# The loads of Q, K and V on ScalarE's queue in place of SyncE's

## The chip, the cores and the metric

The kernel runs on one core of a Trainium2 chip. The metric is the device time of one execution in microseconds (us). The engines are TensorE (PE; its weight loads are PEld), VectorE (DVE), ScalarE (ACT), GpSimd (POOL) and SyncE (SP), which computes nothing and issues DMAs.

## The reference

Attention with a delta rule over 768 tokens, for 4 batches of 8 heads of size 48, then a mixture of 8 experts with a capacity, then a gated two-layer network over all 3072 tokens:

```python
for t in range(S):
    kt, vt, bt = (k_n[:, :, t], v[:, :, t], beta[:, :, t, None])
    y[:, :, t] = np.einsum('bhd,bhde->bhe', q[:, :, t], state)
    v_old = np.einsum('bhde,bhd->bhe', state, kt)
    state = state + bt[:, :, :, None] * np.einsum('bhd,bhe->bhde', kt, vt - v_old)
...
logits = x @ w_gate          # each token to one expert, at most N // E tokens each
h = np.maximum(x[mask] @ w1[e], 0.0); out[mask] = h @ w2[e]
...
h = x @ w_in; g = h * (1.0 / (1.0 + np.exp(-h))); y = g @ w_out
```

`k_n` is K divided by its norm along the head.

## The kernel before

The tokens are cut into 24 chunks of 32, and the state is carried from chunk to chunk. Numbers are split into pairs of float16 (a high and a low part), so each product takes three matmuls.

`prep(c)` loads a chunk's Q and K, transposed, in two halves of 128 x 512 float32 (256 KB each) into one of three `raw` buffers (line 351; the first four chunks are loaded whole, line 344) and splits each half: ACT makes the high part (L353), DVE the low part (L354). For a pair of chunks four DMAs then copy K inside SBUF into `gsl` (L359). `gram(c)` multiplies K and Q with K (L376). `tgroup(g)`, once for four chunks, solves a triangular system on DVE and POOL (L443 and L446, with L429, L449 and L458 around them). `stage(c)` loads K and V once more, not transposed, in one DMA of 384 KB into one of two buffers `kr` (line 466), splits K (L469 on ACT, L470 on DVE), scales V (L473), and then copies all the matmul weights of the chunk with four DMAs of 256 KB inside SBUF into `rsl[x]`, of which there are two (L482). `step(c)` is the recurrence: V goes into PSUM (L505), the old state is multiplied in (L513, L523), the result is split on ACT and DVE (L487, L488), more matmuls follow (L534, L549, L560), some splits use ACT twice (L492, L495), and every second chunk leaves by four DMAs (L572). `gate(c)` makes the expert logits. The MoE begins after the last chunk; it is bound by the matmuls of L1124. The conversion of `win` (L787 loads it) is spread through the end of attention.

No engine's order is written by hand. Every operation is given to `Plan.op` with an engine, a cost, what it reads and writes and a priority. `Plan.order` simulates the engines and puts all operations in one list by their planned starts; the engines then run their parts of it strictly in order. A DMA whose engine is SP also needs one of eight lanes in this plan:

```python
if o[6] and e == "SP":
    s = max(s, lanes[0])
```

The DMAs of SP, in the order in which they are issued, tell of their landing through eight semaphores in turn (DMAHW0 to DMAHW7 in the lists of instructions below). A DMA that takes over a semaphore waits until the one that had it before has landed.

Of the kernel before, what the change touches and what calls it, by code (L numbers as in the profile page):

```python
# [237 lines left out]
def dve(n):  # L238
    return 0.15 + 0.00104 * n


def act(n, sb=True):
    return 0.165 + 0.00083 * n + (0.03 if sb else 0.0)


def pool(n):
    return 0.22 + 0.0018 * n
# [6 lines left out]
def attention(tc, P, ar, sh, kq, kv, bt, cst, idh, wg, xs):  # L254
    nc = tc.nc
# [24 lines left out]
    kr = [ar.new([("kr", i), ("kv", i, 0)], [16, D]) for i in two]  # L280
# [25 lines left out]
    def nat(x, a, t):  # L306
        return NAT[x] + 2 * a + t

    def blk(h):
        return slice(32 * h, 32 * h + 32)  # L310

    def dma(nbytes, fn, r, w, cost=0.63, slots=None, **k):
        P.op("SP", cost, fn, r=r, w=w, lat=0.9, xfer=slots or nbytes / 360e3, **k)

# [13 lines left out]
    late = [("cp", 0, x, k) for x in two for k in ("h1", "l1")]  # L328
# [6 lines left out]
    def grams(c):  # L335
        return (rsl[1][:, 0:8].rearrange("p (x c) g s n -> p x c g s n", x=2), ("rsl", 1)) if c in (2, 3) else (gsl, "gsl")

    def prep(c):
        m, x = c // 2, c % 2
        gs, gk = grams(c)  # L340
        cr = [cpt[m % NR][:, x, r[x]:r[x] + 4].rearrange("p (l t) n -> p l t n", l=2) for r in (QR, KR)]
        ck = lambda k: ("cp", m % NR, x, k)
        if c < 4:
            dma(5.25e5, lambda e: nc.sync.dma_start(first[c][0].rearrange("p k n -> p (k n)"), kq[c]), [], first[c][1])
        for k in (1, 0):
            if c < 4:
                rt, rk = first[c][0][:, k], first[c][1]
            else:
                i = (2 * c + 1 - k) % 3
                rt, rk = raw[:, i], [("raw", i)]  # L350
                dma(2.62e5, lambda e, rt=rt, k=k: nc.sync.dma_start(rt, kq[c, :, 512 * k:512 * k + 512]), late if c < 8 else [], rk)
            rt = rt.rearrange("p (t n) -> p t n", t=2)
            P.op("ACT", act(512), lambda e, k=k, rt=rt: A.activation(cr[k][:, 0], rt, AF.Copy, scale=2.0 ** 9), r=rk, w=[ck(f"h{k}")])  # L353
            P.op("DVE", dve(512), lambda e, k=k, rt=rt: V.scalar_tensor_tensor(cr[k][:, 1], rt, 2.0 ** 9, cr[k][:, 0], op0=OP.mult,  # L354
                                                                               op1=OP.subtract), r=rk + [ck(f"h{k}")], w=[ck(f"l{k}")])
        if x:
            def slots(e):
                for h in range(4):
                    nc.sync.dma_start(gs[blk(h)].rearrange("p x c g s n -> p (x c g) s n")[:, :, h],  # L359
                                      cpt[m % NR][blk(h)].rearrange("p x c (g n) -> p (x c g) n", g=2)[:, 2 * KR[0]:2 * KR[0] + 16])  # L360
            dma(5.25e5, slots, [("cp", m % NR, y, k) for y in range(2) for k in ("h1", "l1")], [gk], cost=2.6, pieces=4, slots=2.5)
# [99 lines left out]
    def stage(c):  # L461
        gi = next(g for g, cs in enumerate(GROUPS) if c in cs)
        m, x = c // 2, c % 2
        cr, k_ = cpt[m % NR][:, x], kr[x]
        ck = lambda k: ("cp", m % NR, x, k)
        dma(3.93e5, lambda e: nc.sync.dma_start(k_.rearrange("p a d -> p (a d)"), kv[c]), late if c < 2 else [], [("kr", x), ("kv", x, 0)])
        hi, lo = (cr[:, nat(x, a, 0):nat(x, a, 2)].rearrange("p t (g n) -> p (t g) n", g=2)[:, :, 0:2 * D] for a in two)
        src = k_[:, 0:8].rearrange("p (b a) d -> p b (a d)", b=4)
        P.op("ACT", act(384), lambda e: A.activation(hi, src, AF.Copy, scale=2.0 ** 9), r=[("kr", x)], w=[ck("nh")])  # L469
        P.op("DVE", dve(384), lambda e: V.scalar_tensor_tensor(lo, src, 2.0 ** 9, hi, op0=OP.mult, op1=OP.subtract),  # L470
             r=[("kr", x), ck("nh")], w=[ck("nl")])
        vs = k_[:, 8:16]
        P.op({"DVE": dve(384), "Pool": pool(384)}, 0, lambda e: E[e].tensor_tensor(  # L473
            vs, vs, nrt[:, gi, c % 4, :, None].to_broadcast([128, 8, D]), op=OP.mult), r=[("nrt", gi)], w=[("kv", x, 0)])
        v2 = vhl[x]
        P.op("ACT", act(384), lambda e: A.activation(v2[:, 0], vs, AF.Copy), r=[("kv", x, 0)], w=[("kr", x)])
        P.op({"DVE": dve(384), "Pool": pool(384)}, 0, lambda e: E[e].tensor_tensor(v2[:, 1], vs, v2[:, 0], op=OP.subtract),
             r=[("kv", x, 0)], w=[("kr", x)])

        def slots(e):  # L480
            for h in range(4):
                nc.sync.dma_start(rsl[x][blk(h)].rearrange("p a g s n -> p (a g) s n")[:, :, h], cr[blk(h)].rearrange("p a (g n) -> p (a g) n", g=2))  # L482
        dma(1.05e6, slots, [ck(k) for k in ("h0", "l0", "h1", "l1", "n", "nh", "nl", "ph", "pl", "th", "tl")],
            [("rsl", x)], cost=2.6, pieces=4, slots=5.1)
# [145 lines left out]
    for c in range(NCH):  # L630
        if c % 2 == 0 and c + 5 < NCH:
            pair(c + 4)
        if c % 4 == 2 and c + 2 < NCH:
            at(c + 2, "tgroup")
            tgroup(c // 4 + 1)
        at(c, "stage")
        stage(c)
        at(c, "step")
        step(c)
        at(c, "gate")  # L640
        gate(c)
# [563 lines left out]
def _program(ins):  # L1205
    import concourse.bacc as bacc

    nc = bacc.Bacc("TRN2", target_bir_lowering=False, num_devices=1)
    d = {k: nc.dram_tensor(f"in_{k}", a.shape, mybir.dt.from_np(a.dtype), kind="ExternalInput").ap()
         for k, a in ins.items()}  # L1210
    out = nc.dram_tensor("out_0", _OUT, F32, kind="ExternalOutput").ap()
    with tile.TileContext(nc) as tc, ExitStack() as ctx:
        dram = ctx.enter_context(tc.tile_pool(name="dram", bufs=1, space=DRAM))
        xs = dram.tile([NTOK, 2 * DM], F16, name="xs")
        plan = Plan()
        ar = Arena(ctx, tc, plan, 212832)
        ar.at(210852)
        sh = shared_tiles(ar)
        ar.at(0)
        plan.base, plan.look = 9.0 * HOT, LOOK  # L1220
        attention(tc, plan, ar, sh, d["kq"], d["kv"], d["bt"], d["cst"], d["idl"], d["wg"], xs)
        moe(tc, plan, ar, sh, xs, d["w1"], d["w2"], d["win"], d["wout"], d["mch"], out)
        with tc.manual_schedule():
            plan.emit()
    return nc
# [22 lines left out]
```

## Time and profile before

| | |
|---|---|
| median of 3 runs | 1058.98 us (1054.76 to 1065.01) |
| the profiled execution's own time | 1058.44 us |
| its span, first to last instruction | 1056.7 us |
| mean granted TensorE clock | 0.934 |

The profiled execution is 0.5 us from the median, and 1.7 us of it lie outside the span. Attention fills about the first 370 us of the span: the last chunk's output is issued at 371 us. Between 350 and 400 us the search for the first expert begins.

### The profile page before, as it was taken

What the parts mean: (1) busy time and instruction counts of PE and PEld (TensorE: products, weight loads), DVE (VectorE), ACT (ScalarE), POOL (GpSimd) and SP (SyncE); (2) the same over time, 40 slices, a digit from 0 to 9 for tenths busy, and PEclk for the clock granted to TensorE, in tenths of its full rate; (3) what the DMA queues carried; (4) which work ended last, traced back from release to release, by engine and by line L of the source; (5) the groups of instructions that cost most, each with busy time, mean ns of one, the idle gap of its engine ahead of it and who ended that gap; (6) DMA issues with size and microseconds to landing.
All of it is one profiled execution on the core that took longest, in us unless ns stands there. A gap on an engine that the chain in (4) does not pass through costs nothing.

```text
span 1056.7 us, 26434 instructions
## 1 busy us (share of the span) xinstructions
PE 921.0 (87%) x10753; PEld 662.3 (63%) x10753; DVE 728.5 (69%) x1831; ACT 493.2 (47%) x992; POOL 444.2 (42%) x567
## 2 busy tenths in 40 slices
PE   7878789898888725987989998997999999999997
PEld 7767779888877613543655654654665666566664
DVE  5999999999974798997477468359459457542250
ACT  4414546464646634555445255236236346741250
POOL 6768676867643241674135035017016113112021
PEclk9987889899988956997999999999999999999999
DMA  7339787888869726213131022004004104401000
GB/s 219 106 77 199 166 190 170 199 190 192 186 158 195 176 76 232 90 61 106 59 105 46 16 63 87 16 10 137 20 1 127 39 1 150 135 1 38 8 1 23
DMA packets 178792, 107.63 MB, mean 102 GB/s; under 512 B 141680, under 2 KB 162416, under 8 KB 178672
## 3 DMA queue, kind: packets, MB, share of 16 engines
q1 hardware_dynamic: 175600, 96.52, 36.0%
q0 software_dynamic: 3072, 9.44, 2.7%
q8 instruction: 84, 1.38, 0.5%
q14 instruction: 36, 0.29, 0.1%
HBM read 65.04 MB, written 9.44 MB: 70 GB/s over the span
## 4 chain that ended last, share of the span: by engine, by line
PE 49%; DVE 23%; DMA 11%; SPq 6%; issue 5%; POOL 4%; ACT 3%; POOLq 0%; DVEq 0%; ACTq 0%
PE bank L1124 41%; SPq L482 4%; DMA sb<-sb 3%; DMA sb<-in_kq 3%; DVE sb L903 3%; DMA sb<-in_kv 2%; DVE sb L443 2%; DVE sb L1164 1%; DMA sb<-xs,sb 1%; DVE sb L1161 1%; DVE sb L446 1%; DVE sb L354 1%; PE bank L192 1%; DVE sb L488 1%; PE bank L376 1%
## 5 line engine op out<-in xcount | busy, mean ns | idle before, releaser
L1124 PE MATMUL bank<-sb 128*128 128x384 f16 x3456 | 591.1, 329 | 6.3 <-DVE sb L1164 5.0
L1124 PEld LDWEIGHTS <-sb 128*128 128x128 f16 x3456 | 327.5, 98 | 220.4 <-issue 8.4
L1164 POOL TENSOR_TENSOR sb<-sb 128x384 f16<-128x384 f32 x71 | 70.4, 996 | 273.1 <-ACT sb L1163 206.3
L1163 ACT ACTIVATE sb<-sb 128x384 f16<-128x384 f32 x128 | 66.1, 520 | 41.7 <-DVE sb L1161 41.1
L1161 DVE SCALAR_TENSOR_TENSOR sb<-bank,sb 128x384 f32<-128x384 f32 x128 | 70.0, 551 | 22.6 <-ACT sb L1160 18.2
L376 PE MATMUL bank<-sb 128*128 128x64 f16 x1152 | 75.3, 242 | 10.5 <-DVE sb L385 5.1
L1160 ACT ACTIVATE sb<-bank 128x384 f32<-128x384 f32 x128 | 61.3, 481 | 47.4 <-PE bank L1124 45.6
L376 PEld LDWEIGHTS <-sb 128*128 128x128 f16 x1152 | 72.8, 120 | 12.2 <-issue 11.0
L1173 POOL DMA_INDIRECT out<-sb x24 | 23.8, 990 | 119.9 <-ACT sb L1171 107.0
L446 POOL TENSOR_TENSOR sb<-sb 128x126 f32<-128x126 f32 (+22 forms) x146 | 68.9, 472 | 10.4
L443 POOL TENSOR_TENSOR sb<-sb 128x126 f32<-128x126 f32 (+22 forms) x146 | 68.1, 466 | 10.4
L443 DVE TENSOR_TENSOR sb<-sb 128x30 f32<-128x30 f32 (+23 forms) x180 | 65.7, 365 | 3.3
L446 DVE TENSOR_TENSOR sb<-sb 128x30 f32<-128x30 f32 (+23 forms) x180 | 63.1, 351 | 3.3
L488 DVE SCALAR_TENSOR_TENSOR sb<-bank,sb 128x192 f16<-128x192 f32 (+1 forms) x118 | 49.7, 426 | 21.1 <-ACT sb L487 20.8
L513 PE MATMUL bank<-sb 128*128 128x48 f16 x1104 | 46.2, 195 | 19.8 <-DMA sb<-sb 12.6
L487 ACT ACTIVATE sb<-bank 128x192 f16<-128x192 f32 (+1 forms) x118 | 45.4, 388 | 37.6 <-PE bank L513 18.7
L513 PEld LDWEIGHTS <-sb 128*128 128x128 f16 x1104 | 43.6, 117 | 23.1 <-issue 21.8
L903 DVE TENSOR_TENSOR sb<-sb 128x192 f16<-128x192 f16 (+3 forms) x116 | 55.3, 512 | 1.0
L1052 POOL TENSOR_TENSOR sb<-sb 128x768 f16<-128x768 f32 x26 | 47.1, 1825 | 20.9 <-ACT sb L1051 20.0
L549 PE MATMUL bank<-sb 128*128 128x48 f16 x1104 | 49.9, 196 | 6.5 <-ACT sb L487 3.8
L1134 ACT ACTIVATE sb<-bank 128x384 f16<-128x384 f32 x64 | 31.3, 489 | 50.7 <-PE bank L1124 46.7
L1135 DVE SCALAR_TENSOR_TENSOR sb<-bank,sb 128x384 f16<-128x384 f32 x64 | 35.3, 554 | 28.0 <-ACT sb L1134 27.9
(159 smaller groups left out, 1494.1 us busy)
## 6 DMA issues: line engine op xcount, KB each, us to landing
sb<-sb SPq DMA_DIRECT2D x96, 256.0 KB, 5.5
sb<-in_w SPq DMA_DIRECT2D x64, 384.0 KB, 4.0
sb<-in_kq SPq DMA_DIRECT2D x40, 256.0 KB, 4.1
sb<-in_kv SPq DMA_DIRECT2D x24, 384.0 KB, 5.2
sb<-sb SPq DMA_DIRECT2D x48, 128.0 KB, 2.7
sb<-in_win SPq DMA_DIRECT2D x8, 768.0 KB, 4.7
sb<-in_wout SPq DMA_DIRECT2D x8, 768.0 KB, 6.5
xs<-sb SPq DMA_DIRECT2D x48, 96.0 KB, 3.9
```

What stands on the lines that cost most here:

```text
L376: T.matmul(gp_[:, Q], sta(gs[:, x], 2 * a + t, Q), cv[:, :, b, t, Q // 4, :, Q % 4], start=(n == 0), stop=(n == 5))
L443: P.op(en, cost[en](n * m), lambda e, x=x, t=t, j=j, n=n, m=m: E[e].tensor_tensor(t, L[:, j:j + 1, j + 1:].to_broadcast([128, n, m]), x[:, ...
L446: P.op(en, cost[en](n * m), lambda e, x=x, t=t, j=j: E[e].tensor_tensor(x[:, :, j + 1:], x[:, :, j + 1:], t, op=OP.add), r=[("tmp", en)], ...
L488: P.op("DVE", dve(n), lambda e: V.scalar_tensor_tensor(lo, src, s, hi, op0=OP.mult, op1=OP.subtract), r=[r, wh], w=[wl])
L513: T.matmul(wu_[:, 0, Q], sta(rs, KR[x] + 2 * a + t, 4 * g + Q), n_[:, b, t, Q, :], start=False, stop=(last and (a, b) == P3[-1] and Q == 3 ...
L549: T.matmul(st_[:, t, Q], sta(rs, nat(x, a, t), 4 * g + Q), u_[:, b, Q], start=(c == 0 and n == 0 and Q == 0 and t == 0), stop=False, skip_ ...
L903: V.tensor_tensor(mv, a, iota2[:, None, 0:J].to_broadcast([128, h, J, 2]), op=o)
L1124: T.matmul(bk[:, :N], lw(a), rw(b), start=(first and n == 0), stop=(last and n == 2))
L1160: op("ACT", act(N, False), lambda e, bk=bk, y=y: A.activation(sg[y], bk[:, :N], AF.Sigmoid, scale=s3), [kbk], [("sg", y)])
L1161: v(dve(N), lambda e, bk=bk, y=y: V.scalar_tensor_tensor(gf[y], bk[:, :N], s3 * 2.0 ** SG, sg[y], op0=OP.mult, op1=OP.mult), [kbk, ("sg", ...
L1163: op("ACT", act(N), lambda e, f=f, y=y: A.activation(gT[:, 0, f], gf[y], AF.Copy), [("gf", y)], [("gT", f, 0)])
L1164: op({"DVE": dve(N), "Pool": pool(N)}, 0, lambda e, f=f, y=y: EN[e].tensor_tensor(gT[:, 1, f], gf[y], gT[:, 0, f], op=OP.subtract), [("gf" ...
```

## The change

The 40 half loads of Q and K (all but those of the first four chunks) and the 24 loads of K and V are issued by ACT. A new helper gives them to the plan at a cost of 0.1 us, where SP's DMAs had 0.63 us, and without lanes. What they load, their buffers and what they wait for stay. SP keeps the copies inside SBUF, the outputs and all loads of the MoE.

```diff
+    def load(nbytes, fn, r, w):
+        P.op("ACT", 0.1, fn, r=r, w=w, lat=0.9, xfer=nbytes / 360e3)
+
     def dma(nbytes, fn, r, w, cost=0.63, slots=None, **k):
         P.op("SP", cost, fn, r=r, w=w, lat=0.9, xfer=slots or nbytes / 360e3, **k)
...
-                dma(2.62e5, lambda e, rt=rt, k=k: nc.sync.dma_start(rt, kq[c, :, 512 * k:512 * k + 512]), late if c < 8 else [], rk)
+                load(2.62e5, lambda e, rt=rt, k=k: nc.scalar.dma_start(rt, kq[c, :, 512 * k:512 * k + 512]), late if c < 8 else [], rk)
...
-        dma(3.93e5, lambda e: nc.sync.dma_start(k_.rearrange("p a d -> p (a d)"), kv[c]), late if c < 2 else [], [("kr", x), ("kv", x, 0)])
+        load(3.93e5, lambda e: nc.scalar.dma_start(k_.rearrange("p a d -> p (a d)"), kv[c]), late if c < 2 else [], [("kr", x), ("kv", x, 0)])
```

Three lines are added, so a line L351 of before is L354 of the changed kernel, L353 is L356, L466 is L469, L469 is L472, L482 is L485, L487 is L490, and so on. Since the plan is made anew, all engines' orders change in attention; after it, from the expert search on, the five orders are the same as before. The numbers of instructions stay, but for the 64 DMAs and four small operations that the plan gives to another of their permitted engines.

SP's queue of the kernel before, from the output of chunks 0 and 1 (L572) past that of chunks 2 and 3 (the next L572):

```order
L572 DMA xs<-sb 32x8x192 x4
L351 DMA sb<-in_kq 128x512 x2
L359 DMA sb<-sb 32x16x128 x4
L466 DMA sb<-in_kv 128x768
L482 DMA sb<-sb 32x32x128 x4
L351 DMA sb<-in_kq 128x512 x4
L482 DMA sb<-sb 32x32x128 x4
L466 DMA sb<-in_kv 128x768
L572 DMA xs<-sb 32x8x192 x4
L466 DMA sb<-in_kv 128x768
L359 DMA sb<-sb 32x16x128 x4
L482 DMA sb<-sb 32x32x128 x4
```

The same place in the changed kernel, where L575 is the output, L362 the copy for `gsl` and L485 the copy for `rsl`:

```order
L575 DMA xs<-sb 32x8x192 x4
L362 DMA sb<-sb 32x16x128 x4
L485 DMA sb<-sb 32x32x128 x8
L575 DMA xs<-sb 32x8x192 x4
L362 DMA sb<-sb 32x16x128 x4
L485 DMA sb<-sb 32x32x128 x8
```

The copies of one chunk now follow those of the chunk before with nothing between them; the nine loads that stood among them are gone from this queue.

ACT's order of the kernel before, between the splits of the outputs of chunk 1 (bank 70) and chunk 2 (bank 69), with what each instruction waits for in brackets (an engine's name is that engine's semaphore):

```order
L487 ACTIVATE sb<-bank_67 128x192 [waits DVE_49,PE_49]
L492 ACTIVATE sb<-bank_68 128x192 [waits DVE_49,PE_49]
L389 ACTIVATE sb<-sb 128x256 [waits DVE_49]
L353 ACTIVATE sb<-sb 128x512 [waits DMAHW5_49,DMAHW4_49,DMAHW6_49,DMAHW3_49,DMAHW1_49]
L469 ACTIVATE sb<-sb 128x4x96 [waits DMAHW7_49]
L383 ACTIVATE sb<-bank_71 128x8x32 [waits PE_49]
L495 ACTIVATE sb<-bank_68 128x192 [waits PE_49]
L487 ACTIVATE sb<-bank_65 128x384 [waits Activation_49]
```

The same place in the changed kernel:

```order
L490 ACTIVATE sb<-bank_67 128x192 [waits DVE_49,PE_49]
L386 ACTIVATE sb<-bank_71 128x8x32 [waits DVE_49]
L495 ACTIVATE sb<-bank_68 128x192 [waits PE_49,Activation_49]
L392 ACTIVATE sb<-sb 128x256
L354 DMA sb<-in_kq 128x512 [waits DVE_49,Activation_49]
L356 ACTIVATE sb<-sb 128x512 [waits DMAHW6_49,DMAHW4_49,DMAHW7_49,DMAHW2_49,DMAHW0_49]
L472 ACTIVATE sb<-sb 128x4x96 [waits DMAHW1_49]
L386 ACTIVATE sb<-bank_71 128x8x32 [waits PE_49]
L354 DMA sb<-in_kq 128x512 [waits DMAHW3_49,DVE_49]
L490 ACTIVATE sb<-bank_65 128x384 [waits PE_49]
```

The eight semaphores of the DMAs now go round over the DMAs of both queues. Two loads stand among ACT's own operations. Both wait for DVE, the second one also for the DMA that had DMAHW3 before it, which may be one of SP's; behind it stands the split of the state (L490 on bank 65), for which the next chunk's matmuls wait.

## Rows read from the trace of the kernel before

**Rows 1.** The page, parts 1 (busy time, share, instructions) and 4 (the chain).

```profile
PE 921.0 (87%) x10753; PEld 662.3 (63%) x10753; DVE 728.5 (69%) x1831; ACT 493.2 (47%) x992; POOL 444.2 (42%) x567
...
PE 49%; DVE 23%; DMA 11%; SPq 6%; issue 5%; POOL 4%; ACT 3%; POOLq 0%; DVEq 0%; ACTq 0%
PE bank L1124 41%; SPq L482 4%; DMA sb<-sb 3%; DMA sb<-in_kq 3%; DVE sb L903 3%; DMA sb<-in_kv 2%; DVE sb L443 2%; DVE sb L1164 1%; DMA sb<-xs,sb 1%; DVE sb L1161 1%; DVE sb L446 1%; DVE sb L354 1%; PE bank L192 1%; DVE sb L488 1%; PE bank L376 1%
```

**Rows 2.** Busy time by stretch: PE, PEld, DVE, ACT, POOL, clock, DMA share.

```profile
100.00:150.00 50.00, 40.87 (x918) 39.60 (x916) 45.78 (x117) 25.21 (x63) 34.06 (x60) 0.85 0.79 177
150.00:200.00 50.00, 44.03 (x1010) 42.61 (x1009) 46.43 (x118) 28.03 (x68) 37.49 (x66) 0.91 0.80 178
200.00:250.00 50.00, 43.75 (x1039) 42.51 (x1037) 47.85 (x124) 29.01 (x71) 36.41 (x63) 0.97 0.82 195
250.00:300.00 50.00, 43.60 (x1079) 42.33 (x1077) 44.36 (x116) 28.73 (x69) 33.14 (x66) 0.95 0.81 180
300.00:350.00 50.00, 39.58 (x979) 37.53 (x976) 31.40 (x78) 28.03 (x66) 14.83 (x21) 0.87 0.90 183
```

**Rows 3.** The chain by line, from 100 to 250 us.

```profile
by line: SPq L482 15.7%; DMA sb<-in_kq 13.5%; DMA sb<-sb 7.3%; issue 7.1%; DMA sb<-in_kv 6.0%; DVE sb L488 4.5%; SPq L572 3.8%; DVE sb L443 3.5%; DVE sb L354 3.2%; ACT sb L353 2.8%; DVE sb L449 2.7%; DVE sb L446 2.6%; SPq L359 2.0%; SPq L35
```

**Rows 4.** The chain by line, from 250 to 350 us.

```profile
by line: SPq L482 18.8%; DMA sb<-sb 18.8%; DMA sb<-in_kv 12.1%; PE bank L549 4.8%; PE bank L523 4.3%; issue 4.0%; DVE sb L470 3.2%; DVE sb L488 3.0%; PE bank L376 3.0%; PE bank L560 2.5%; DVE sb L443 2.2%; POOL sb L443 2.2%; DVE sb L449 2.2
```

**Rows 5.** Line 351, the half loads: duration ns min/median/max; time to landing.

```profile
L351 SPq DMA_DIRECT2D sb<-in_kq x40: 327/436/2298, 13.5 to 242.2; - x40
...
DMA to landing us min/median/max: 2.6/4.1/6.5
```

**Rows 6.** Line 466, the loads of K and V, the same way.

```profile
L466 SPq DMA_DIRECT2D sb<-in_kv x24: 327/430/1722, 15.6 to 336.0; - x24
...
DMA to landing us min/median/max: 3.3/5.2/6.4
```

**Rows 7.** Lines 482, 359 and 572, SP's other DMAs in attention, the same way.

```profile
L482 SPq DMA_DIRECT2D sb<-sb x96: 585/1176/5140, 75.4 to 350.4; - x96
...
L359 SPq DMA_DIRECT2D sb<-sb x48: 597/635/1645, 7.3 to 252.6; - x48
...
L572 SPq DMA_DIRECT2D xs<-sb x48: 325/468/2272, 107.6 to 371.4; - x48
```

**Rows 8.** SP's waits, 50 to 350 us: us in total, times, longest.

```profile
SPq L351 <- DVE sb L354: 31.6, 7, 21.2
SPq L466 <- PE bank L505: 11.8, 5, 5.5
...
SPq L351 <- DVE sb L443: 6.0, 5, 2.0
...
SPq L351 <- DVE sb L488: 3.4, 2, 2.2
```

**Rows 9.** SP's queue, 38 to 66 us: start, length, what, count.

```profile
41.74 0.33 SPq L466 DMA_DIRECT2D sb<-in_kv  x1
63.94 0.33 SPq L351 DMA_DIRECT2D sb<-in_kq  x1
```

**Rows 10.** The chain's pieces from 200 to 410 us: start, length, what.

```profile
286.90 6.16 DMA sb<-in_kv
...
303.30 1.60 SPq L482
...
305.68 1.22 SPq L482
307.01 5.93 DMA sb<-in_kv
313.02 0.54 ACT sb L469
```

**Rows 11.** The computing engines' waits for loads, 50 to 350 us, the same way.

```profile
POOL sb L473 <- DMA sb<-in_kv: 29.1, 8, 9.1
...
ACT sb L353 <- DMA sb<-in_kq: 19.5, 6, 10.7
...
ACT sb L469 <- DMA sb<-in_kv: 14.1, 14, 2.6
```

## The prediction, made before the changed kernel was run

> **What bounds the kernel now.** The page comes first. TensorE is busy for 87% of the span and the chain of work that ended last is 41% matmuls of L1124, the MoE, to which the change does nothing [rows 1]. So whatever it brings lies in attention, the first 370 us. The same chain spends 6% on SP's queue and 3% and 2% on the loads of K and Q and of K and V [rows 1], and these are all in attention.
>
> Next the busy times by stretch. From 100 to 250 us VectorE works 45.8, 46.4 and 47.9 us of every 50; only 4.2, 3.6 and 2.2 us of it are idle, 9.9 us in all [rows 2]. The DMA engines are at 0.79 to 0.82 and ScalarE at a little over half. From 250 to 300 VectorE still has 44.4, and from 300 to 350 only 31.4, while the DMA share rises to 0.90 [rows 2]. So attention has two parts: one in which VectorE is nearly full, and a tail in which the copies and the recurrence take turns.
>
> Then the chain by line in these two parts. From 100 to 250 us SP's issues and the transfers are about half of it: L482 15.7%, the half loads 13.5%, copies 7.3%, the loads of K and V 6.0%, L572 3.8%, L359 2.0% [rows 3]. From 250 to 350 us it is L482 with 18.8%, the copies with 18.8%, the loads of K and V with 12.1% [rows 4]. The reader is to see that the loads are on the chain in both parts, but that in the first VectorE is just behind them.
>
> **The change part by part.**
>
> *SP's own time.* 40 issues of 436 ns and 24 of 430 ns (medians) leave SP: 27.8 us [rows 5, 6]. With them go the waits that stood in front of the loads: 31.6 us for L354, of which one of 21.2 us lies between 42.1 and 63.9 us, before the first L482 at 75.4, where no copy stands behind it [rows 7 to 9]; without it 10.4. Then 6.0 and 3.4 us for other operations of VectorE, and 11.8 for L505 [rows 8]: 31.6 us. By itself none of this is on the path, since SP computes nothing; it counts where a copy or a load comes earlier.
>
> *The loads land earlier.* A half load takes 4.1 us from issue to landing in the median and 2.6 at best, a load of K and V 5.2 and 3.3 [rows 5, 6]. From 100 to 250 us the half loads are on the chain for 13.5% of 150 us, 20.3 us in four pieces, and the others for 9.0 us in two [rows 3]. At their best they would take 10.4 and 6.6, so at most 12.3 us are to be had. VectorE is late next: it can give back only its 9.9 idle us [rows 2]. SP and the transfers hold some 48% of this chain and the loads 19.5 of these 48 points [rows 3], so I take 41% of the 9.9 us: 4.0 us. The bounds are 0 and 9.9.
>
> In the tail two loads of K and V are on the chain, 6.16 and 5.93 us long; at 3.3 us each that is 5.5 us to gain. The second one could be issued only after SP had done L482, from 303.30 to 307.01 us: another 3.7 [rows 10]. Together 9.2 us, and VectorE has room here (5.6 and 18.6 us idle) [rows 2]. What is late next are the copies into `rsl`, which hold three times the chain that the loads do [rows 4] and which cannot go before the step two chunks back has read its buffer. I take half, 4.6 us; the bounds are 0 and 9.2.
>
> *What ACT pays.* No DMA of ACT is in the trace. The nearest rows are the same loads on SP, 0.33 us at the shortest and 0.43 in the median [rows 5, 6]; the plan reckons 0.1 us. Below zero it cannot be: ACT gets instructions and loses none but a small one. I take 0.43, since the loads are the same 128 rows, so 27.8 us of ACT's queue. To this come the waits of 31.6 us, which now stop ACT in place of SP: behind each load ACT's next operation is queued, at the place shown the split of the state, for which TensorE's matmuls of the next chunk wait. 59.4 us in all, 0.93 per load, put into the idle time of an engine that is busy for 57% at most in these stretches [rows 2]. What of it is on the path? The chain holds 3% of the span on ACT, 32 us, of its 493.2 busy us [rows 1], one part in 15. So I take 59.4 / 15 = 4.0 us. The lower bound is the issues alone, 27.8 / 15 = 1.9; the upper one counts the stalls whenever ACT would have worked, 57% of 59.4, 34 us.
>
> *New order.* VectorE's and POOL's instructions change by two operations each; nothing to price. After the search the orders are the same, so the 650 us of the MoE move with its start and not in length.
>
> The sum: 4.0 + 4.6 saved, 4.0 paid, 4.6 us less than the profiled execution's 1058.44 us, which is **1054 us**. Against the median of the runs, 1058.98, it is 0.5% less. About 1%, 10.6 us, is what a measurement of this kernel can tell from no change: its three runs span 10 us.
>
> **The rivals.**
>
> *A, faster: SP was the gate.* L482 took 1176 ns per DMA in the median where 585 are possible [rows 7], and SP's part of the chain is larger than that of the loads [rows 3, 4]. If taking nine loads from between the copies lets both gains reach their bounds, 9.9 + 9.2 = 19.1 us, with ACT paying the issues alone, 1.9, the time is 1041 us. For it: L482, the copies and the loads hold 42.5% and 49.7% of the chain in the two parts [rows 3, 4]. Against it: VectorE at 93% up to 250 us [rows 2], and copies that are held by the DMA engines stay as long. The Trainium skill, "DMA: Bandwidth & Descriptors", section "Queues, rings and completion order", says that each DMA engine goes round between the queues that have work, packet by packet, with one queue for SP and one for ACT; by it a load on ACT's queue would pass the copies that wait on SP's. No run here shows two such queues, since before all of this went through one; by this rule the loads would land near 3.3 us and the sum would move toward A.
>
> *B, slower: ACT's queue is held.* SP is issuing for much of the time: 96 x 1.176 + 48 x 0.635 + 48 x 0.468 = 166 us of the 296 between the first L482 and the last L572, 56% [rows 7]. If a DMA of ACT has to wait while SP is in one, it waits half of 1.18 us in 56% of the cases, 0.33 us, 21 us for all 64. ACT would then pay 59.4 + 21 = 80 us, 1.25 per load. The place is the one shown in the lists: a load in front of a split that the recurrence needs. With one load in three there (between 1 in 15 and the 57% of ACT's busy share), it is 27 us, less the 8.6 gained: 1058.4 + 18 = 1076 us. From that share of one in three on, a load that holds ACT for 0.40 us eats the whole gain (0.40 x 64 / 3 = 8.6), and the issue alone has 0.43. For it: L351 has taken up to 2.3 us to issue on SP [rows 5]. Against it: ACT idles some 21 us or more in every 50 [rows 2], and much of that it waits in front of the very operations that the loads feed: 19.5 + 14.1 us, and POOL 29.1 [rows 11]. The Trainium skill, "Perfetto Trace Analysis", section "DMA Instruction — HWDGE (DVE, Sync)", says that one descriptor generator is shared by the two sequencers that issue such DMAs, that a DMA locks it for itself until its descriptors are made, and that the wait for the lock is part of the DMA's reported time. That would be B's mechanism; the trace of before, with one issuer, cannot show it.
>
> *C, it does not do what it says.* A DMA waits until the one that had its semaphore before has landed, whoever issued that; the eight go round over both queues, so a load on ACT waits for the DMA eight places before it, mostly a copy of SP's. Where that ends last, the loads come no earlier, and ACT has the waits: 1058.4 + 4 = 1062 us.
>
> **How the numbers follow.** The forecast, 1054 us with its own spread of 1045 to 1063, has 0.40; A 0.26; B 0.25; C 0.09. Faster by over 1%, below 1048.4 us, are A and 0.07 of the forecast: 0.33. Slower by over 1%, above 1069.6, are B and 0.02 of C: 0.27. Within 1% is the rest, 0.40. The range leaves out the outer part of A and of B, a tenth on either side: from 1039 us, somewhat below A's 1041, to 1078, somewhat above B's 1076.
>
> **What would show it.** In the profile after, ACT's queue has 64 DMA issues. If the forecast is right they take near 0.43 us, the loads land in about 3 to 4 us, the waits of POOL, L353 and L469 for loads shrink from 62.7 us to less than half, VectorE's idle time from 100 to 250 us falls by about 4 us, and the waits of TensorE and VectorE for ACT grow a little. For A, VectorE would be above 97% in these stretches and the last L572 would be issued some 15 us before 371. For B, the issues on ACT take 0.8 us or more, or the idle time of VectorE and TensorE in front of L487's successors grows by some 20 us. For C, the loads on ACT begin when a copy of SP's lands. Wrong would make it: an issue on ACT that costs its engine next to nothing (then A), a granted clock that falls below the 0.85 to 0.97 of these stretches [rows 2], or a start of the MoE that moves while its length moves the other way.

## The result and the profile after

The changed kernel takes 1075.71 us (median of 4 runs, 1073.09 to 1076.72) beside 1060.22 us for the kernel before (4 runs, 1054.76 to 1065.01): 1.0142 times as long, with a 95% interval of 1.0107 to 1.0178, so 15 us more. The profiled execution took 1075.61 us, with a span of 1073.9 us and a granted clock of 0.922.

The page, parts 1 and 4, which answers to [rows 1]:

```profile
PE 925.2 (86%) x10753; PEld 665.4 (62%) x10753; DVE 730.5 (68%) x1832; ACT 495.3 (46%) x991; POOL 440.5 (41%) x567
...
PE 52%; DVE 23%; DMA 12%; issue 4%; POOL 4%; SPq 2%; ACT 2%; POOLq 0%; ACTq 0%; DVEq 0%
PE bank L1127 41%; DMA sb<-sb 6%; DVE sb L906 3%; PE bank L379 3%; DMA sb<-in_kq 2%; PE bank L526 2%; SPq L485 2%; PE bank L516 2%; DVE sb L449 2%; DVE sb L446 2%; DVE sb L1167 1%; PE bank L552 1%; DVE sb L1164 1%; DMA sb<-xs,sb 1%; DMA sb<
```

SP's queue has gone from 6% of the chain to 2%, as the change wants it, and the copies inside SBUF (`DMA sb<-sb`) have gone from 3% to 6%. The engines' busy times hardly moved. L575, the output of attention, tells where the time was lost:

```profile
L575 SPq DMA_DIRECT2D xs<-sb x48: 303/469/2873, 111.0 to 386.4; - x48
```

The last output is issued at 386.4 us and not at 371.4 [rows 7], 15.0 us later. The first is 3.4 us late, so 11.6 us build up between the first output and the last. The busy times by stretch answer to [rows 2] (PE, PEld, DVE, ACT, POOL, clock, DMA share):

```profile
100.00:150.00 50.00, 40.12 (x923) 38.95 (x921) 46.04 (x114) 24.17 (x58) 34.06 (x62) 0.89 0.83 176
150.00:200.00 50.00, 42.92 (x960) 41.45 (x958) 43.66 (x112) 27.75 (x67) 32.41 (x59) 0.84 0.88 177
200.00:250.00 50.00, 41.58 (x926) 40.25 (x924) 41.01 (x108) 25.32 (x61) 31.25 (x59) 0.82 0.81 162
250.00:300.00 50.00, 42.49 (x1035) 40.98 (x1032) 45.16 (x118) 27.50 (x68) 33.20 (x64) 0.90 0.80 178
300.00:350.00 50.00, 39.07 (x998) 37.51 (x996) 33.54 (x86) 27.16 (x66) 15.75 (x32) 0.86 0.84 169
```

VectorE works 46.0, 43.7 and 41.0 us from 100 to 250 us: it is idle for 19.3 us in place of 9.9. The chain by line, from 100 to 250 us, answers to [rows 3]:

```profile
by line: DMA sb<-sb 16.8%; PE bank L379 8.2%; issue 6.9%; DMA sb<-in_kq 4.6%; PE bank L526 4.2%; SPq L485 4.1%; DVE sb L357 4.1%; DVE sb L491 4.1%; POOL sb L446 3.7%; POOL sb L449 3.6%; DMA xs<-sb 3.6%; DMA sb<-in_kv 3.6%; DVE sb L446 2.6%;
```

And from 250 to 350 us, to [rows 4]:

```profile
by line: DMA sb<-sb 30.0%; SPq L485 8.7%; PE bank L516 8.6%; PE bank L526 8.0%; PE bank L552 7.2%; DMA sb<-in_kv 5.0%; issue 3.7%; PE bank L537 3.6%; PE bank L563 3.3%; DVE sb L491 2.5%; DVE sb L449 2.2%; DVE sb L446 2.0%; PE bank L584 1.8%
```

The loads fell from 19.5% to 8.2% of the first and from 12.1% to 5.0% of the second; the copies rose from 7.3% to 16.8% and from 18.8% to 30.0%. The same exchange stands in the waits of the computing engines, 50 to 350 us (us in total, times, longest). Those for loads answer to [rows 11]:

```profile
ACT sb L356 <- DMA sb<-sb: 30.3, 14, 3.8
...
PE bank L516 <- DMA sb<-sb: 20.3, 10, 5.0
...
PEld L516 <- DMA sb<-sb: 11.1, 4, 5.2
...
POOL sb L476 <- DMA sb<-in_kv: 9.9, 3, 4.1
...
ACT sb L472 <- DMA sb<-in_kv: 0.8, 2, 0.6
```

Waiting for loads shrank from 62.7 us to 10.7. Waiting for copies grew: ACT in front of the split L356, whose buffer an earlier copy still reads, and TensorE in front of L516, whose weights a copy brings. The kernel before had for these two, at its lines L353 and L513:

```profile
PE bank L513 <- DMA sb<-sb: 9.1, 8, 2.2
ACT sb L353 <- DMA sb<-sb: 8.0, 5, 2.3
```

So the loads are in time now and the copies are late. One thing that makes copies late is seen in SP's waits, 50 to 365 us:

```profile
SPq L485 <- DMA sb<-in_kv: 15.6, 5, 4.7
...
SPq L485 <- DMA sb<-in_kq: 8.7, 6, 3.0
...
SPq L362 <- DMA sb<-in_kq: 4.5, 4, 2.6
SPq L362 <- DMA sb<-in_kv: 3.6, 2, 2.1
...
SPq L575 <- DMA sb<-in_kv: 1.5, 1, 1.5
```

These are five ways in which a DMA inside SBUF, or an output, waits for a load of K, Q or V: 33.9 us in all, where the kernel before had 1.9 in the same stretch:

```profile
SPq L351 <- DMA sb<-in_kq: 1.9, 1, 1.9
```

Each wait is counted whole and put down to what ended it, so 33.9 us is the most that the loads can have cost SP in this stretch. One of these waits, in SP's queue (start, length, what, count):

```profile
116.53 2.50 SPq L362 DMA_DIRECT2D sb<-sb  x3
123.84 4.40 SPq L485 DMA_DIRECT2D sb<-sb  x4
```

and on ACT at the same time:

```profile
118.14 0.33 ACTq L469 DMA_DIRECT2D sb<-in_kv  x1
...
123.77 0.52 ACT L472 ACTIVATE sb<-sb 128x384 f16<-128x384 f32 x1 [0.28 <-DMA sb<-in_kv]
```

SP finished its three L362 at 119.03 us and then stood until 123.84. The copy it was about to issue does not need what it waited for: the load issued at 118.14 landed as ACT's L472, its first reader, started at 123.77, and the copy started 0.07 us later, before L472 was done. In the changed kernel's list of instructions this copy is the one that has to take over the semaphore DMAHW5, and the load had it. The eight semaphores go round over both queues: a load that is in flight on ACT's queue stops SP if a copy is next in turn, although the copy has nothing to do with it. Two such stops lie on the chain that ended last. It has three pieces of a load between 95 and 390 us; these two end in the issue of a copy by SP (L362 and L485), and the copy's transfer follows:

```profile
97.25 6.92 DMA sb<-in_kq
...
189.52 5.38 DMA sb<-in_kv
...
195.54 7.27 DMA sb<-sb
```

The issue itself is cheap. L354 and L469 answer to [rows 5, 6]:

```profile
L354 ACTq DMA_DIRECT2D sb<-in_kq x40: 334/335/1851, 8.7 to 251.0; - x40
L354 ACTq EVENT_SEMAPHORE  x23: 17/17/8214, 14.4 to 249.3; - x23
...
DMA to landing us min/median/max: 2.7/3.8/7.4
```

```profile
L469 ACTq DMA_DIRECT2D sb<-in_kv x24: 334/335/864, 10.2 to 351.5; - x24
...
DMA to landing us min/median/max: 3.1/4.6/6.5
```

334 ns at the least and 335 in the median, which would be 21.4 us for 64; with the few long ones, up to 1851 ns, it is 25.6 us. ACT's longest wait in front of a load is 8.2 us. The loads landed in 3.8 and 4.6 us in place of 4.1 and 5.2. The copies, L485, answer to [rows 7]:

```profile
L485 SPq DMA_DIRECT2D sb<-sb x96: 585/968/3092, 77.8 to 364.8; - x96
...
DMA to landing us min/median/max: 3.4/5.8/8.5
```

They took 5.8 us to land, where the page of the kernel before has 5.5 for them. For the copies of L362, half as large, it is 4.0 us in place of 2.7.

### The profile page after: what moved, and what is told of

The parts are those of the page before. It is cut to its first block, busy times and chain, and to the rows that moved or that the text cites. A ratio compares the mean times of both kernels' runs of the same rounds, so it can differ in the third digit from the quotient of the medians.

```text
span 1073.9 us, 26407 instructions
## 1 busy us (share of the span) xinstructions
PE 925.2 (86%) x10753; PEld 665.4 (62%) x10753; DVE 730.5 (68%) x1832; ACT 495.3 (46%) x991; POOL 440.5 (41%) x567
## 4 chain that ended last, share of the span: by engine, by line
PE 52%; DVE 23%; DMA 12%; issue 4%; POOL 4%; SPq 2%; ACT 2%; POOLq 0%; ACTq 0%; DVEq 0%
PE bank L1127 41%; DMA sb<-sb 6%; DVE sb L906 3%; PE bank L379 3%; DMA sb<-in_kq 2%; PE bank L526 2%; SPq L485 2%; PE bank L516 2%; DVE sb L449 2%; DVE sb L446 2%; DVE sb L1167 1%; PE bank L552 1%; DVE sb L1164 1%; DMA sb<-xs,sb 1%; DMA sb<-in_kv 1%
## 5 line engine op out<-in xcount | busy, mean ns | idle before, releaser
L379 PEld LDWEIGHTS <-sb 128*128 128x128 f16 x1152 | 72.8, 120 | 15.7 <-issue 14.1
L449 POOL TENSOR_TENSOR sb<-sb 128x126 f32<-128x126 f32 (+22 forms) x146 | 68.9, 472 | 10.5
L490 ACT ACTIVATE sb<-bank 128x192 f16<-128x192 f32 (+1 forms) x118 | 46.1, 392 | 52.1 <-PE bank L516 27.6
L516 PE MATMUL bank<-sb 128*128 128x48 f16 x1104 | 47.0, 198 | 25.8 <-DMA sb<-sb 20.3
L446 POOL TENSOR_TENSOR sb<-sb 128x126 f32<-128x126 f32 (+22 forms) x146 | 63.5, 435 | 10.0
L491 DVE SCALAR_TENSOR_TENSOR sb<-bank,sb 128x192 f16<-128x192 f32 (+1 forms) x118 | 49.9, 426 | 24.7 <-ACT sb L490 24.5
L516 PEld LDWEIGHTS <-sb 128*128 128x128 f16 x1104 | 43.5, 117 | 28.2 <-issue 16.9
```

What stands on the lines that cost most here:

```text
L379: T.matmul(gp_[:, Q], sta(gs[:, x], 2 * a + t, Q), cv[:, :, b, t, Q // 4, :, Q % 4], start=(n == 0), stop=(n == 5))
L446: P.op(en, cost[en](n * m), lambda e, x=x, t=t, j=j, n=n, m=m: E[e].tensor_tensor(t, L[:, j:j + 1, j + 1:].to_broadcast([128, n, m]), x[:, ...
L449: P.op(en, cost[en](n * m), lambda e, x=x, t=t, j=j: E[e].tensor_tensor(x[:, :, j + 1:], x[:, :, j + 1:], t, op=OP.add), r=[("tmp", en)], ...
L491: P.op("DVE", dve(n), lambda e: V.scalar_tensor_tensor(lo, src, s, hi, op0=OP.mult, op1=OP.subtract), r=[r, wh], w=[wl])
L516: T.matmul(wu_[:, 0, Q], sta(rs, KR[x] + 2 * a + t, 4 * g + Q), n_[:, b, t, Q, :], start=False, stop=(last and (a, b) == P3[-1] and Q == 3 ...
```

## Experiments

Three theories in the end: T, the loads cost ScalarE's time; S1, the semaphores that two queues share stop SP's copies; S2, the loads' bytes on a second queue run beside the copies and make them land later. The first runs still had Q (the queue, whatever it is) against O (the new order). "SP's waits" below are those for loads, 50 to 365 us, summed from the list of waits; "the outputs' time" runs from the first to the last output DMA of attention.

**The two halves of the change.** The changed order on every engine, all loads on SP's queue:

```diff
-load(..., lambda e: nc.scalar.dma_start(...), ...)
+load(..., lambda e: nc.sync.dma_start(...), ...)
```

> The changed kernel's plan, so the same order on PE, DVE, ACT and POOL, but the 64 loads are issued by SP again. Theory Q (ACT's queue pays: the issues, the waits in front of them and the shared semaphores cost the time): near the kernel before, 1060 us, at most 1065. Theory O (the new order costs it: the plan now puts the splits of Q and K, L356, so early that ACT stands there until a copy of SP's has landed): near the changed kernel, 1070 to 1080, with L356 still waiting some 25 to 35 us for copies (30.3 in the changed kernel, 8.0 for L353 before).

1068.5 us, 1.0054 (1.0031 to 1.0076). SP's waits are gone and the outputs take 264.7 us, against 263.8 before:

```profile
L575 SPq DMA_DIRECT2D xs<-sb x48: 308/462/1369, 110.4 to 375.1; - x48
```

And the other half, the order of before with `nc.scalar.dma_start` in its two `dma` calls:

> The plan and so the order of the kernel before, but the 64 loads are issued by ACT, at the places that the plan gives them among ACT's operations. Theory Q: near the changed kernel, 1072 to 1080. Theory O: near the kernel before, 1054 to 1064, with the waits of L353 for copies near the 8 us of before.

1082.7 us, 1.0206 (1.0183 to 1.0228). SP's waits are 32.7 us, mostly these, and the outputs take 276.7 us:

```profile
SPq L482 <- DMA sb<-in_kq: 17.4, 7, 5.2
...
SPq L482 <- DMA sb<-in_kv: 9.4, 2, 5.0
...
SPq L572 <- DMA sb<-in_kv: 4.0, 2, 3.1
```

The first time lies between the two theories and the second above both. The order alone is 6 us of the 15, and putting the loads on ACT's queue in that order adds the larger part. In the old order the queue costs even more, 1.0206 in all.

**Cures by the plan.** The planner is told that `rsl`'s copy ends 3.5 us later:

```diff
+P.op("SP", 0.0, lambda e: None, r=[("rsl", x)] + [ck(k) for k in (...)], lat=3.5)
```

> The changed kernel, with one thing told to the plan: the chunk buffers that the copies into rsl read become free 3.5 us later than it reckons (an empty operation that reads them). Theory O: the waits of L356 for copies fall from 30 us to 12 or less, and the time by 5 to 12 us, to 1064 to 1071. Theory Q: within 4 us of the changed kernel's 1075.7.

1.0267 (1.0249 to 1.0284). Then, that a load costs ACT 0.335 us in place of 0.1:

> The changed kernel, with the loads planned at 0.335 us each, the time that an issue on ACT was measured to take, in place of 0.1. Theory Q, if it is the issue time: the plan makes room for it and 3 to 10 us come back, 1066 to 1073. Theory O: no change beyond what a new order gives, 1071 to 1080.

1.0204 (1.0163 to 1.0246). And, after the runs below, that a load on ACT takes one of eight lanes too:

```diff
-if x and e == "SP":
+if x and e in ("SP", "ACT"):
```

> The changed kernel, and the planner now counts a load on ScalarE's queue among the transfers that take turns on eight places, as it has always counted SP's (two conditions of the planner take ACT beside SP). All loads stay on ScalarE's queue; the order moves. Theory S1: SP's waits for loads fall from 41 us to under 20, and the time falls below 1.0142, toward 1.0054. Theory S2 and T: the planner knows nothing new that matters, 1.0142 or, as with the two earlier changes of the plan, up to 1.027.

1.0200 (1.0147 to 1.0253); SP's waits are 27.4 us. None of these helps. In the last one S1 had SP's waits under 20 us and a time below 1.0142, and neither came. Each of these plans moved the order, and each new order had its own 27 to 38 us of SP's waits, so these runs don't separate the theories.

**ScalarE's time alone.** Order of after, loads on SP, and in each load's place a throwaway copy on ACT:

```diff
+A.activation(wz[:, 0:160], wz[:, 160:320], AF.Copy)
```

> Changed order kept, all 64 loads on SP, and at each place where ScalarE issued a load it does a throwaway copy of 160 columns instead (about 0.336 us, waits for nothing). This prices ScalarE's time of issue alone: no load on its queue, no wait for a free buffer, no shared semaphore. Theory T1 (the issue time is the cost): near 1.0142, at least 1.011, with 21 us more busy time on ScalarE. Theory W (ScalarE's waits in front of the loads) and theory S (semaphores and landing times): near 1.0054, at most 1.008.

1.0102 (1.0036 to 1.0168); the outputs' time is 266.7 us. The copy does wait for something: it writes into `wz`, which TensorE's warm-up (L192) reads, and ACT waits 15.7 us for that. The first output comes at 114.5 us, 4.1 us later than in the order-only run. The same, writing into the buffer of the load:

> As the run before, but the throwaway copy writes 160 (153) columns of the very buffer that the load then fills, so ScalarE waits at each of the 64 places until the buffer is free, as it did in front of a load; the load itself is SP's. Theory T1 or W (ScalarE's time, its waits included): near 1.0142. Theory S: what is missing to 1.0142 here is the semaphores' and the queues' part; were these all of it, the time would stay near 1.0054 to 1.008, and SP's waits for loads near 2 us in place of 41 us.

1.0075 (1.0045 to 1.0106); the outputs' time is 267.1 us. (The 41 us of SP's waits in this expectation are counted from the start of the span; 33.9 us of them lie between 50 and 365 us.) By this second run ACT's issues and waits are worth some 2 us over the order alone, not the 9 that are missing; the intervals of the two runs and of the order-only run overlap.

**Parts of the loads.** Two splits by kind, the loads that stay on SP given to `dma` again:

> Changed order kept, only the 24 loads of K and V in stage() on ScalarE's queue, the 40 half loads back on SP. The two ends known: no load on ScalarE's queue in this order 1.0054 of the time before, all 64 on it 1.0142. Theory T (the loads cost ScalarE's time: 0.335 us of issue each, and its waits in front of them): 24 of 64 issues, 8 us of the 21, so about 1.0054 + 0.375 x 0.0088 = 1.009. Theory S (copies on SP wait for loads on the other queue that held the same one of eight completion semaphores): SP's waits for in_kv keep their 20 us of the 34 us, so about 1.0054 + 0.6 x 0.0088 = 1.0105, and SP's waits for in_kq are gone.

> Changed order kept, only the 40 half loads in prep() on ScalarE's queue, the 24 loads of K and V back on SP. Theory T: 40 of 64 issues, 13 us of ScalarE's time, so about 1.0054 + 0.625 x 0.0088 = 1.011. Theory S: SP's waits for in_kq keep their 13 us of 34 us and those for in_kv go, about 1.0054 + 0.4 x 0.0088 = 1.009. The two splits together should add up to the whole (0.0088) if the loss is a sum over loads; if either alone has nearly all or hardly any of it, one load or one wait decides.

1.0167 (1.0103 to 1.0230) and 1.0109 (1.0050 to 1.0168). The expectation was wrong about what these kernels are: `dma` tells the plan other costs than `load`, so the order moved, and they say nothing of a sum. With the order truly held (only `nc.scalar` and `nc.sync` exchanged), the half loads alone on ACT's queue:

> The changed order on every engine, only the 40 half loads in prep() on ScalarE's queue, K and V back on SP (in the earlier split K and V were also planned as SP's, which moved the order). SP waits for in_kq alone. If the loss is a sum over loads: about 1.0054 + 0.4 to 0.6 x 0.0088 = 1.009 to 1.011, and with the run after this one 0.0088 in all. If SP's loads of K and V now also stand behind copies that wait for half loads (theory S1, one more queue member hurt), up to 1.0142.

1.0171 (1.0124 to 1.0218), with these waits of SP:

```profile
SPq L485 <- DMA sb<-in_kq: 13.1, 4, 5.2
...
SPq L362 <- DMA sb<-in_kq: 9.0, 3, 4.6
...
SPq L575 <- DMA sb<-in_kq: 5.9, 2, 5.1
```

and K and V alone:

> The changed order on every engine, only the 24 loads of K and V in stage() on ScalarE's queue, the half loads back on SP. A sum over loads: about 1.009 to 1.0105. Theory T: 24 of 64 issues, at most 1.007. Theory S1: SP's waits for in_kv stay at 15 to 20 us and hold up SP's half loads too, so 1.010 or more.

1.0107 (1.0078 to 1.0136), with 18.4 us of SP's waits. The half loads alone make the loss as large as all loads do, so the loss doesn't look like a sum over loads. The copies of L485 landed in 5.6 us with the half loads and 5.4 with K and V on ACT's queue, against 5.4 in the order-only run and 5.8 in the changed kernel; those of L362 in 2.9 and 3.3, against 3.1 and 4.0.

**Turns without bytes.** Order of after, loads on SP, and a DMA of 4 bytes on ACT's queue in each place:

```diff
+nc.scalar.dma_start(words[0:1, 3 * c + k:3 * c + k + 1], kq[c, 0:1, 0:1])
```

First with the words in `wz`, which TensorE's warm-up reads:

> Changed order kept, all 64 loads on SP, and at each place where ScalarE issued a load it issues a DMA of 4 bytes into a word of its own instead (it waits for no buffer and moves no data worth the name). So ScalarE's queue has its 64 issues of about 0.335 us and its 64 turns on the eight completion semaphores, but none of the 20 MB. Known: this order with SP's loads 1.0054; with a throwaway copy in each place 1.0102 (no wait) and 1.0075 (with the buffer's wait). Theory S1 (the semaphores that two queues share): at least 1.012, with SP waiting tens of us in front of copies for DMAs of a few bytes, and ScalarE waiting in front of its spots for copies. Theory S2 (the loads' 20 MB on a second queue, beside the copies) and theory T (ScalarE's time): 1.0054 to 1.010, as with the throwaway copies.

1.0244 (1.0191 to 1.0296), as S1 had it, but not for its reason. TensorE waits for the small DMAs in its warm-up:

```profile
PE bank L192 <- DMA sb<-in_kq: 20.0, 11, 2.5
```

The first output comes at 126.4 us. SP's waits are 12.5 us, and the outputs' time is 264.3, no longer than in the order-only run. With a tile of their own:

> The DMA of 4 bytes on ScalarE's queue at each of the 64 places again, into words of a tile that nothing else touches, so the start is free of it; all loads on SP, changed order kept. In the earlier run the outputs of the pairs were issued over 264 us, as with no such DMA (265 us; 275 us in the changed kernel), and the 16 us more had been lost before the first. Theory S1 as a count of turns (each turn of another queue on the eight semaphores costs): near 1.014 or more. S1 by the time that a load is in flight (a copy waits 3 to 5 us because the load takes that long to land, and a few bytes land at once), theory S2 and theory T: 1.0054 to 1.008.

1.0069 (1.0044 to 1.0094). Turns alone cost next to nothing, though these DMAs don't land at once either: SP's waits are 10.6 us, 9.9 of them for the small DMAs (2.2 us at the longest), and the outputs' time is 268.7. S1 as a count of turns is out.

**Turns beside the loads.** The same small DMAs, in front of the loads of the changed kernel:

> The changed kernel, all 64 loads on ScalarE's queue, and in front of each a DMA of 4 bytes on the same queue into words of its own. With loads on SP these 64 extra turns cost 0.15% (1.0069 against 1.0054). Theory S1: more turns bring the load in flight nearer to the copy that gets its semaphore, so SP's waits for loads rise well over the 34 us of the changed kernel, and the time goes over 1.0142 by clearly more than 0.0015: at least 1.020. Theory S2: no byte and no queue is added, about 1.0157.

1.0272 (1.0212 to 1.0332). S1 said at least 1.020, S2 1.0157. So 64 small DMAs that cost 1.6 us where the loads are SP's (1.0069 against 1.0054) cost 13.8 us where the loads are ACT's too (1.0272 against 1.0142). SP's waits rose from 33.9 to 50.0 us, mostly these:

```profile
SPq L489 <- DMA sb<-in_kv: 16.7, 6, 5.0
SPq L489 <- DMA sb<-in_kq: 15.7, 9, 4.5
SPq L366 <- DMA sb<-in_kq: 14.4, 10, 2.4
```

and the outputs' time from 275.4 to 283.8 us, with the first output 5.9 us later:

```profile
L579 SPq DMA_DIRECT2D xs<-sb x48: 303/470/2313, 116.9 to 400.7; - x48
```

The small DMAs read K and Q as the half loads do, so these lines hold both. By the line that issued the DMA waited for, 34.7 us are for the loads, hardly more than the 33.9, and 15.3 us for the small DMAs, 3.6 us at the longest. So S1 had the time and the sum of the waits right, and not that SP would wait longer for the loads themselves. What the 64 more issues cost ACT beside the loads isn't told apart from these waits.

**Semaphores of their own.** K and V on GpSimd's queue, which doesn't take part in the eight (its DMAs have semaphores of their own in the list of instructions), and the control in which GpSimd fills the buffer for about as long as an issue took (0.58 us) and SP loads:

```diff
-nc.sync.dma_start(k_.rearrange("p a d -> p (a d)"), kv[c])
+nc.gpsimd.dma_start(k_.rearrange("p a d -> p (a d)"), kv[c])        # or, in the control:
+G.memset(k_.rearrange("p a d -> p (a d)")[:, 0:560], 0.0), nc.sync.dma_start(...)
```

> Changed order kept, the 40 half loads on SP, the 24 loads of K and V on GpSimd's queue, which has completion semaphores of its own. On ScalarE's queue these 24 loads took the kernel from 1.0054 to 1.0167. Theory S1: SP's waits for in_kv (28 us with ScalarE's queue) are gone, and the time is near 1.0054, more only by what GpSimd pays for the issues. Theory S2 (a second queue lets loads run beside the copies, which land later for it): the second queue is still there, so near 1.0167, with the copies of L485 landing as late. Theory T: no time of ScalarE, near 1.0054. If GpSimd's issues are dear and held up, its own work in front of VectorE slows and the run can't tell.

> Changed order kept, all 64 loads on SP, and GpSimd does a throwaway fill of 560 columns of the K/V buffer at each of the 24 places where it issued the load of K and V (about 0.58 us each, with the same wait until the buffer is free). If the 1.0141 with K and V on GpSimd's queue was GpSimd's own time and waits (then theory S2 has nothing from that run, and S1 stands), this is near 1.0141, at least 1.011. If it was the bytes on a second queue (theory S2), this stays near 1.0054 to 1.008.

1.0141 (1.0087 to 1.0195) and 1.0066 (1.0047 to 1.0085). The 1.0167 of the first expectation is from the split whose order moved; with the order held, K and V on ACT's queue gave 1.0107. The same for the half loads:

> The changed order on SP, ScalarE, VectorE and TensorE, the 24 loads of K and V on SP, the 40 half loads on GpSimd's queue (completion semaphores of its own). On ScalarE's queue these 40 gave 1.0171, with SP waiting 28 us for them. Theory S1: no such wait is left, so the time falls to that of the next run, its control. Theory S2: the bytes are still on a second queue, so about 0.009 to 0.012 over the control.

> Control of the run before: all 64 loads on SP in the changed order, and GpSimd fills the half load's buffer (512 columns, about 0.53 us, with its wait until the buffer is free) at each of the 40 places. It gives GpSimd's time alone, 21 us of fills and its waits: 1.0054 to 1.015 by both theories (24 such fills for K and V gave 1.0066).

1.0142 (1.0101 to 1.0183) and 1.0084 (1.0054 to 1.0114). In all four SP waits for no load, so the 0.6 to 0.75% between each pair is not S1; S1 had said that both runs on GpSimd's queue fall to their controls. The outputs' time says the same. K and V on GpSimd's queue, then the half loads:

```profile
L575 SPq DMA_DIRECT2D xs<-sb x48: 308/465/1880, 108.4 to 382.6; - x48
L575 SPq DMA_DIRECT2D xs<-sb x48: 309/459/1839, 111.4 to 387.4; - x48
```

274.2 and 276.0 us, as long as the 275.4 of the changed kernel, against 267.2 and 263.7 in the controls. The copies land later beside a second queue. L485 with the half loads on GpSimd's queue:

```profile
L485 SPq DMA_DIRECT2D sb<-sb x96: 585/1246/4334, 78.4 to 365.7; - x96
...
DMA to landing us min/median/max: 3.4/5.9/8.5
```

and in its control:

```profile
L485 SPq DMA_DIRECT2D sb<-sb x96: 585/1106/3987, 80.3 to 356.4; - x96
...
DMA to landing us min/median/max: 3.4/5.4/6.5
```

For K and V those of L485 don't (5.5 against 5.6 us). The smaller copies of L362 do in both pairs: 4.6 us against 3.1 with K and V on GpSimd's queue, 5.2 against 3.8 with the half loads. S2 is therefore likely for GpSimd's queue and not settled in its mechanism.

## Why the prediction was wrong

It forecast 1054 us and the time is 1075.71, inside its range and on the other side. It gave 0.27 to a time slower by over 1%. That the range reaches so far is due to rival B, whose mechanism isn't the one at work, so it was luck.

**The term that was missing: ACT's loads make SP's copies late.** "The sum: 4.0 + 4.6 saved, 4.0 paid" has no cost for SP at all; "SP's own time" only takes 27.8 us of issues and 31.6 us of waits away from it. Rival C had the shared semaphores, but in one direction: a load on ACT that waits for a copy. The other one is what the trace shows: SP waits 33.9 us for loads, where it had waited 1.9, and the copies' share of the chain goes from 7.3% to 16.8% and from 18.8% to 30.0%. All runs with the order of after:

| run | SP's waits for loads and small DMAs, us | outputs' time, us | ratio |
|---|---|---|---|
| order only | 0 | 264.7 | 1.0054 |
| throwaway copies on ACT, into `wz` | 0 | 266.7 | 1.0102 |
| throwaway copies on ACT, into the buffers | 0 | 267.1 | 1.0075 |
| fills on GpSimd at the places of K and V | 0 | 267.2 | 1.0066 |
| fills on GpSimd at the places of the half loads | 0 | 263.7 | 1.0084 |
| small DMAs on ACT, loads on SP | 10.6 | 268.7 | 1.0069 |
| small DMAs on ACT into `wz`, loads on SP | 12.5 | 264.3 | 1.0244 |
| K and V on ACT | 18.4 | 269.5 | 1.0107 |
| half loads on ACT | 28.4 | 275.4 | 1.0171 |
| the changed kernel | 33.9 | 275.4 | 1.0142 |
| small DMAs and loads on ACT | 50.0 | 283.8 | 1.0272 |
| K and V on GpSimd | 0 | 274.2 | 1.0141 |
| half loads on GpSimd | 0 | 276.0 | 1.0142 |

The first two numbers of a row are from one profiled execution; the runs without any such wait and without a load on a second queue lie between 263.7 and 267.2 us. Where loads are on ACT's queue, the outputs' time rises with SP's waits: 0.38 us for each us from the order-only run to the last of them ((283.8 - 264.7) / 50.0). With the order of before it is 0.42 ((276.7 - 263.8) / (32.7 - 1.9)). ACT's own time, some 2 us, is in these numbers. That S1 is at work the trace shows, with two of its stops on the chain that ended last; that it costs this much is read from the slope.

That S1 is all of it isn't shown. The last two rows take as long as the changed kernel without any such wait, so loads on a second queue can make the copies late by themselves, on GpSimd's queue at least. On ACT's queue the copies' landing moved from 5.4 to 5.8 us (L485) and from 3.1 to 4.0 (L362) between the order-only run and the changed kernel. How much of the 9 us that the queue costs is S1 and how much the bytes on a second queue stays open. Loads on ACT's queue with semaphores of their own would tell; they weren't tried, and in every kernel here the eight go round over both queues.

**"New order: nothing to price."** Wrong: the order alone costs 5.7 us (0.0054 of 1060), though the numbers of instructions stay. In that run ACT waits 19.0 us in front of L356 for copies, where the kernel before had 8.0: the plan put the splits earlier, with loads that it takes for nearly free, and they run into copies that still read their buffers. Whether that wait is all of the 5.7 us wasn't shown. In its profiled execution the last output is only 3.7 us later than before (375.1 against 371.4), and 2.8 of these lie before the first output (110.4 against 107.6).

**"The loads land earlier", 8.6 us saved.** They did (4.1 to 3.8 and 5.2 to 4.6 us), and the engines' waits for them fell to a sixth, further than the "less than half" that was foretold. Nothing of it reached the end: VectorE's idle time from 100 to 250 us, of which it was to give back 4 us, grew from 9.9 to 19.3 us, because the copies are late next. The text names them as late next in the tail, but as something that stays; the change made them later.

**"What ACT pays", 4.0 us.** Near the 2 us of the second throwaway run and the 5 of the first, which are not told apart from one another (the first one started later). The issue was 0.335 us in the median, not 0.43. ACT's largest share in [rows 2] is 58% (29.01 us of 50), not 57.

**Rival B** gave 1076 us, but for a reason that isn't there: few issues on ACT are held (334 ns at the least, 335 in the median; B wanted 0.8). All 64 took 25.6 us, 4.2 more than 64 times 334 ns, where B had 21 more. VectorE's wait for the split of the state, B's other sign, hardly grew (18.4 to 19.3 us from 50 to 350 us, L491 for L490). Its 56% is too high as well: 20 of the 48 issues of L359 come before the first L482, and without them it is 52%. The wait for the lock of one descriptor generator would, by the Trainium skill, "Perfetto Trace Analysis", section "DMA Instruction — HWDGE (DVE, Sync)", be part of the issue's reported duration; this trace doesn't show it in the median, though the longest issue took 1.85 us. **Rival A** fails on the copies as well. The Trainium skill, "DMA: Bandwidth & Descriptors", section "Queues, rings and completion order", says that each DMA engine goes round between the queues that have work; from this the prediction took that the loads would pass the waiting copies and land near 3.3 us. In the changed kernel the trace agrees in direction (3.8 and 4.6 us, where the order-only run has 4.2 and 4.9). With only the half loads or only K and V on ACT's queue it shows no gain: 4.2 and 4.9 us. Either way a load that passes gains little and the copies lose more.

**The granted clock**, named as a way to be wrong, did fall below its range: 0.84 and 0.82 from 150 to 250 us, where it had been 0.91 and 0.97 [rows 2]. TensorE was busy for 42.9 and 41.6 us of these two stretches, where it had been for 44.0 and 43.8. It looks like a small part: over the five stretches a matmul takes 42.6 ns in the mean (206.2 us for 4842) in place of 42.2 (211.8 us for 5025), 2 us in all.

## What to carry to other kernels

When a DMA moves to another engine's queue, list what the two queues still share. Here eight completion semaphores go round over both, and a queue that used to run in line waits for the other one's transfers: look in SP's waits for DMAs that the waiting instruction doesn't read. With the loads on ACT's queue the time rose by 0.4 us for each us of such waits, while 52 us less waiting for loads bought nothing, since the copies were next. That the time rises with a wait doesn't make the wait the whole cause: on GpSimd's queue the wait was gone and the loss stayed. And a change of the queue that is also a change of the plan has to be timed in two halves: the new order alone was more than a third of the loss (5.7 of 15.5 us).

## What the runs showed of the hardware

An issue on ScalarE's queue took 335 ns in the median for 256 and for 384 KB, less than the 436 and 430 ns on SP; at the least it is 334 ns against 327, and the longest took 1851 ns. SP's copies took 968 ns in the median at the same time. The eight semaphores go round over the DMAs of SP and ACT, and in the changed kernel SP stood for 33.9 us in front of DMAs that read none of what it waited for. GpSimd's queue with semaphores of its own was no way out: over its control it cost 0.6 to 0.75%, with no wait of SP's for loads.
